# A new instruction order for a one-core attention, FFT and MLP kernel, with its last chunk finished in pieces

## The chip, the core and the metric

The kernel runs on one NeuronCore of a Trainium2 chip. The metric is the device time of one execution in microseconds (us). Engines: TensorE (PE in the profile; PEld is its weight loading), VectorE (DVE), ScalarE (ACT), GpSimd (POOL) and SyncE (SP), which here only issues transfers; "SPq" rows are SP issuing a DMA.

## The reference

Attention over 8 batches and 8 heads (576 positions, head size 64), then a mixing layer and an MLP on the result.

```python
scores = scale * np.matmul(q, k.transpose(0, 1, 3, 2))
mask_local = (rel >= 0) & (rel < 32)                       # heads 0 to 3
mask_strided = (rel >= 0) & (pos[None, :] % 32 == pos[:, None] % 32)   # heads 4 to 7
attn = softmax(np.where(mask, scores, -1e9)); attn_out = np.matmul(attn, v)
x = attn_out.transpose(0, 2, 1, 3).reshape(B, S, H * D)    # 8 x 576 x 512
u = x + np.real(np.fft.fft(np.fft.fft(x, axis=1), axis=2))
un = (u - mu) / np.sqrt(var + 1e-06)                       # over the last axis
return u + np.maximum(un @ w_ch1, 0.0) @ w_ch2             # 512 -> 2048 -> 512
```

## The kernel before, in words

**Attention.** The eight heads of a batch are four pairs; pairs 0 and 1 have the local mask, 2 and 3 the strided one. For each pair a load brings q and k (`qk5_0` is batch 5, pair 0) and the values; TensorE makes the scores (`s`, line 501 for a local pair, 54 small matmuls), DVE and ACT do the softmax, a DMA transpose on SP's queue turns the probabilities (`pT`, line 520, 18 blocks for a local pair), TensorE multiplies them with the values (`o`, lines 532 and 539), and the normalized result goes to `xd` in memory. When a batch's four pairs are there, `xa` loads a part of it back (line 998) and GpSimd gathers the rest by indirect DMAs (line 1002). Batch 0 works another way: its transposes are matmuls (line 754), and SP loads its inputs first of all (`q`, `mstr`, `mloc`, and the values `v` and `vlx`, `vsx`).

**Mixing.** Additions on DVE and GpSimd (`E`, `O`, `FD`, line 1010) and matmuls (`A`, `B`) make the FFTs. The result is normalized (`unp`) and turned by a DMA transpose (`uT`, line 1308).

**MLP.** The 4608 tokens are 18 chunks of 256, c0 to c17. A chunk has eight "ups": 24 matmuls of 128x256 into `ph` (line 1532), which ACT and GpSimd make into an fp16 high and low part. The "downs" (line 1658) are 96 matmuls of 128x512 into two accumulators, `acc`; DVE adds u to them (line 1666), and SP stores the rows (line 1675). The last four chunks make the downs from seven products instead of eight: 168 matmuls of 128x256 (line 1601) into `pa` and `pb`. There every up is followed by `hidden7`: relu on ACT (line 1564) into one of two `x` buffers, four 128x128 sums on DVE (line 1568, "hsum"), an fp16 copy on ACT (line 1575) and the rest of it on DVE (line 1578). `finish7` (lines 1608 to 1611) puts the seven products together: one ACT copy and eight DVE instructions, and then both stores.

**What sets the order.** Every engine carries out its instructions in the order in which they stand in the program, and a waiting instruction holds up all behind it. That order is laid out while the program is built, by a planner in the kernel (class `Order`). Steps are announced as `op(engine, duration, ...)`, with the buffers that they take (`get`) and give back (`put`), the events that they need, a bias and a slack. The planner takes the steps one after another by the time at which their engine could begin them and by their bias; steps with `alt` may go to DVE or GpSimd. SP has a model of its own: how long an issue takes of its queue, and when the transfer engines are free. The numbers that steer all this are the table `P`: biases by kind of step, slacks (`SLD2` is the slack ahead of `o`), `LX` and `LE` (what hsum and `E` on the second engine count extra), `ORD0` (batch 0's pairs in order), `vo` (which value loads of batch 0 stand behind which q load). Where the planner foresees idle TensorE while a PSUM tile for weight statistics is open, it puts in dummy matmuls (line 1381).

Of the kernel before, what the change touches and what calls it, by code (L numbers as in the profile page):

```python
# [11 lines left out]
F32 = mybir.dt.float32  # L12
# [3 lines left out]
AF = mybir.ActivationFunctionType  # L16
# [3 lines left out]
B, H, S, D = 8, 8, 576, 64  # L20

P = dict(
    WV0=0.228, ub=-187.36, SL2=0, SLD2=3.532, GL0=8, LAT=0.637, GL=9.0, t2=121.316, l0=-1127.679, a0=-807.088,
    sq0=-7.328, w00=-751.008, w01=-485.877, w02=-485.971, hold=398.589, c=-935.492, z=175.263, f0=-1280.172,
    w03=-170.758, s00=-640.699, s01=-730.715, s02=-653.813, s03=-436.694, w1=-58.299, s1=-408.163, p0=-1078.153,
    p1=-355.073, pn=-123.274, a1=-327.528, f1=-427.179, a2=80.128, f2=-74.138, an=258.341, fn=153.256, db=-50.784,
    up=323.728, dn=544.434, ev=154.438, WS=1.287, WV=0, WA=0.042, WG=21.908, WT=0, SL=0.222, SLD=0, np=3, AL=116.829,
    SG=57.917, Lcl=-4.074, Lfs=108.137, Lwl=68.096, Lul=-140.163, LO=-208.877, LE=-1.586, Lc2=108.104, LSD=-60.205,
    Lsub=100.369, Lsub0=83.995, Lrt=107.889, Lu=45.646, ORD0=(3, 1, 0, 2), vo=([], [2], [0, 1], [3]),
    S0=('qk', 'qk', 'kt', 'pt'),  # L30
    S1=('f6', 'f6', 'u', 'kt', 'u', 'f6', 'uT', 'u', 'u', 'uT', 'f6', 'f6', 'kt', 'f6', 'f6', 'qk'), HB=4, RB=1, X0=0,
    X1=0, X2=0, cs=187.891, T=-13.32, TQ=3, LT=71.249, LX=13.094, LH=-7.702, LF=27.454,
)
ORD0 = P["ORD0"]
FP32 = {(b, hp) for b in range(3) for hp in range(4)}
# [134 lines left out]
class Op:  # L170

    def __init__(self, engine, dur, get="", put="", need="", sets="", at=None, lat=None, n=1, slack=0.0, dma=0.0, note="", alt=None):
# [25 lines left out]
class Order:  # L200
# [38 lines left out]
    def run(self, until=None):  # L239
        while self.threads and until not in self.events:  # L240
# [44 lines left out]
                    self.cold = est + 3.6  # L285
                o.dur += min(o.dur, max(self.cold - est, 0.0) / 2)
            if o.engine == "S" and o.dur:
                self.free["S"] = est + 0.5 * o.n
                end = self.free["D"] = max(max(est + 1.3, self.free["D"]) + o.dur, est + 0.42 * o.n + 1.1)
            else:  # L290
                end = self.free[o.engine] = est + o.dur
                if o.engine in "VG" and pair(o):
                    h = self.held[o.engine]
                    h.append((est, end - 0.14))
                    del h[:-6]
                if o.dma:
                    end = self.free["D"] = max(est + 2.0, self.free["D"]) + o.dma
# [17 lines left out]
op = Op  # L315
# [3 lines left out]
def body(ctx: ExitStack, tc: tile.TileContext, a, out):  # L319
# [24 lines left out]
    def psbig(name):  # L344
        return big.tile([128, 1024], F32, tag="big", name=name)
# [77 lines left out]
    def att_pair(b, hp):  # L423
# [94 lines left out]
        yield op("S", 2.4 if local else 1.7, lat=2.4, get="pt", need="zv", put="qk" if local else "pbt", note=f"turn {nm}")  # L518
# [72 lines left out]
    def att_pair32(b, hp):  # L591
# [6 lines left out]
        end = yield op("S", 1.7, get="qk vsum" if hp == ORD0[0] else "qk", note=f"load {nm}")  # L598
# [665 lines left out]
    def norm(c, s, u, uT):  # L1264
# [42 lines left out]
        yield op("S", 0.9, put=ptag, sets=f"uT{nm}", note=f"uT {nm}")  # L1307
        nc.sync.dma_start_transpose(uT[:, :, 128 * s : 128 * s + 128], unp.rearrange("p x d -> p (x d)"))


# [150 lines left out]
    def xt(name):  # L1461
        return late_["p"].tile([128, 8, 128], F32, tag="x", name=name, bufs=2)
# [25 lines left out]
    class Chunk:  # L1488


        def __init__(self, c, keys):
            self.c, self.keys = c, keys
            self.h = {}
# [59 lines left out]
        def ups7(self):  # L1553
            c = self.c
            for fp in range(8):
                yield op("T", 2.61, get=("f6" if fp % 2 else "hq") + " ph", put="uT" if fp == 7 else "", sets=f"up{c}" if fp == 7 else "", at=0, note=f"up {c} {fp}", slack=SLD)
                spawn(self.hidden7(fp, self.up_products(fp)), bias=P["ev"])

        def hidden7(self, fp, ph):

            c = self.c
            yield op("A", 0.62, get="x", put="ph", note=f"relu {c} {fp}")
            X = xt(f"x{c}_{fp}")
            A.activation(X[:, 4:8].rearrange("p k t -> p (k t)"), ph, AF.Relu, scale=HS / 2)  # L1564
# [226 lines left out]
```

## Time and profile before

| | us |
|---|---|
| time, median of 3 runs (lowest, highest) | 958.61 (954.17, 961.56) |
| the profiled execution | 956.11 |
| its span | 954.3 |
| PE busy | 915.7 (96%) |
| DVE busy | 667.1 (70%) |
| ACT busy | 475.7 (50%) |
| POOL busy | 273.3 (29%) |

The span is what the trace covers; 1.8 us of the profiled execution lie outside it. TensorE is busy nearly throughout, so the table says little about what a changed order is worth: that stands in the places where TensorE waits, and in the stretches ahead of its first and behind its last product.

### The profile page before, as it was taken

How to read it: one execution, taken by the hardware profiler on the slowest of the kernel's cores; microseconds unless marked ns; L12 is line 12 of the kernel's file. 1: busy time of each engine (PE TensorE's matmuls, PEld its weight loads, DVE VectorE, ACT ScalarE, POOL GpSimd, SP SyncE). 2: the span in 40 equal slices, each digit the busy share in tenths (PEclk: the TensorE clock that was granted, in tenths of full speed). 3: DMA queues.
4: the chain of work that ended last, by engine and by line, in shares of the span. 5: the costliest groups of instructions: out<-in, count | busy, mean ns of one | idle time of the engine just before them, and what ended most of it. 6: DMA issues, size and time to landing. Idle time of an engine off the chain costs nothing.

```text
span 954.3 us, 24166 instructions
## 1 busy us (share of the span) xinstructions
PE 915.7 (96%) x10166; PEld 675.1 (71%) x10166; DVE 667.1 (70%) x1293; ACT 475.7 (50%) x883; POOL 273.3 (29%) x260
## 2 busy tenths in 40 slices
PE   7788999999999999999999999999999999999996
PEld 6666875757776667666766667666767767888885
DVE  4679877586875677569575687759665988657363
ACT  3468763446645546364744565455633454333331
POOL 0101242346422441346332551255224510000000
PEclk9999999999999999999999999999999999999998
DMA  9887562354325850564327451655142101101000
GB/s 284 294 325 268 175 169 81 87 152 123 112 47 124 176 129 29 123 166 95 97 48 164 104 165 21 168 133 138 31 93 78 34 12 40 23 23 45 2 23 23
DMA packets 131885, 105.50 MB, mean 111 GB/s; under 512 B 101089, under 2 KB 109697, under 8 KB 131777
## 3 DMA queue, kind: packets, MB, share of 16 engines
q1 hardware_dynamic: 129296, 95.84, 37.8%
q0 software_dynamic: 2480, 8.13, 3.1%
q8 instruction: 79, 1.29, 0.6%
q14 instruction: 30, 0.24, 0.1%
HBM read 65.23 MB, written 18.89 MB: 88 GB/s over the span
## 4 chain that ended last, share of the span: by engine, by line
PE 59%; DVE 4%; DMA 2%; issue 1%; ACT 1%; POOL 0%; DVEq 0%; ACTq 0%
PE acc L1658 19%; PE ph L1532 18%; PE ph L1549 9%; PE pa L1601 4%; PE pb L1601 3%; PE B L1118 1%; DMA pT<-qk 1%; PE A L1095 1%; PE s L501 1%; PE o L532 1%; DVE unp L1306 1%; PE o L539 1%; DVE tmp L1010 0%; PE A L1096 0%; DMA uT<-unp 0%
## 5 line engine op out<-in xcount | busy, mean ns | idle before, releaser
L1532 PE MATMUL ph<-uT,W 128*128 128x256 f16 x2688 | 308.7, 274 | 2.0 <-DMA uT<-unp 2.0
L1658 PE MATMUL acc<-W,h 128*128 128x512 f16 x1344 | 302.3, 379 | 3.2 <-DVE u L1666 3.2
L1532 PEld LDWEIGHTS <-W 128*128 128x128 f16 x2688 | 259.8, 98 | 40.7 <-DMA uT<-unp 2.1
L1637 POOL TENSOR_TENSOR h<-hf,h 128x512 f16<-128x512 f32 x112 | 142.9, 1276 | 331.0 <-ACT h L1635 247.4
L1658 PEld LDWEIGHTS <-h 128*128 128x128 f16 x1344 | 128.6, 98 | 147.8 <-issue 4.2
L1634 ACT ACTIVATE hf<-ph 128x512 f32<-128x512 f32 x112 | 66.4, 593 | 166.9 <-PE ph L1532 133.7
L1549 PE MATMUL ph<-uT,W 128*128 128x256 f16 x768 | 86.5, 273 | 0.0
L1549 PEld LDWEIGHTS <-W 128*128 128x128 f16 x768 | 75.1, 98 | 9.1
L1601 PEld LDWEIGHTS <-h 128*128 128x128 f16 x660 | 64.6, 98 | 8.8
L1275 POOL TENSOR_TENSOR rstd<-mv,negh 128x1 f32<-128x1 f32 x36 | 26.2, 730 | 149.2 <-DVE mv L1272 142.2
L1635 ACT ACTIVATE h<-ph 128x512 f16<-128x512 f32 x112 | 66.2, 591 | 0.3 <-DVE W L1349 0.3
L1568 DVE TENSOR_TENSOR x<-x 128x128 f32<-128x128 f32 x128 | 31.3, 287 | 34.0 <-ACT x L1564 32.9
L1306 DVE TENSOR_TENSOR unp<-un,unp 128x512 f16<-128x512 f32 x33 | 37.6, 1140 | 24.5 <-ACT unp L1303 24.5
L1578 DVE TENSOR_TENSOR h<-x,h 128x896 f16<-128x896 f32 x32 | 34.8, 1091 | 22.9 <-ACT h L1575 22.7
L1575 ACT CAST h<-x 128x896 f16<-128x896 f32 x32 | 30.0, 938 | 40.0 <-DVE x L1568 38.4
L1564 ACT ACTIVATE x<-ph 128x512 f32<-128x512 f32 x32 | 19.1, 597 | 49.8 <-PE ph L1549 47.1
L478 DVE SCALAR_TENSOR_TENSOR kt<-qk,sc,kt 128x576 f16<-128x576 f32 (+1 forms) x40 | 35.0, 915 | 9.3 <-ACT kt L463 9.3
L463 ACT ACTIVATE kt<-qk,sc 128x576 f16<-128x576 f32 (+1 forms) x40 | 29.3, 785 | 19.1 <-DVE sc L419 12.8
L1254 ACT ACTIVATE pq<-B,fcm 128x128 f32<-128x128 f32 (+7 forms) x105 | 27.2, 380 | 14.4 <-DVE rt L1244 9.5
L1303 ACT CAST unp<-un 128x512 f16<-128x512 f32 x33 | 20.4, 617 | 22.9 <-DVE un L1285 19.1
L1601 PE MATMUL pa<-T,h 128*128 128x256 f16 x192 | 31.4, 273 | 0.0
L1601 PE MATMUL pa<-W,h 128*128 128x256 f16 x184 | 30.5, 273 | 0.0
(298 smaller groups left out, 1352.6 us busy)
## 6 DMA issues: line engine op xcount, KB each, us to landing
qk<-in_qk SPq DMA_DIRECT2D x28, 592.0 KB
sa<-in_w SPq DMA_DIRECT2D x20, 512.0 KB
out<-u SPq DMA_DIRECT2D x32, 256.0 KB
W<-in_w SPq DMA_DIRECT2D x12, 512.0 KB
vn<-in_vl SPq DMA_DIRECT2D x10, 432.0 KB
xd<-xo SPq DMA_DIRECT2D x16, 256.0 KB
vn<-in_vs SPq DMA_DIRECT2D x10, 384.0 KB
xa<-xd SPq DMA_DIRECT2D x7, 512.0 KB
```

The costliest lines, as they stand in the source:

```text
L478: V.scalar_tensor_tensor(out=lo, in0=src, scalar=f, in1=hi, op0=ALU.mult, op1=ALU.subtract)
L1306: on(o).tensor_tensor(out=unp[:, 1], in0=un, in1=unp[:, 0], op=ALU.subtract)
L1532: T.matmul(ph[:, i, :], W1[:, 4 * (f0 // 512) + d, x, f0 % 512 : f0 % 512 + 128], self.uhl[y][:, d, :], start=(n == 0), stop=(n == 11))
L1549: T.matmul(ph[:, 256 * i : 256 * i + 256], W1[:, 4 * (f0 // 512) + d, x, f0 % 512 : f0 % 512 + 128], self.uhl[y][:, d, :], start=(n == 0), ...
L1568: on(o).tensor_tensor(out=X[:, k], in0=X[:, x], in1=X[:, y], op=f)
L1575: A.copy(h[:, 0], X[:, 0:7])
L1578: on(o).tensor_tensor(out=h[:, 1], in0=X[:, 0:7], in1=h[:, 0], op=ALU.subtract)
L1601: T.matmul(ps[:, 256 * q : 256 * q + 256], h[:, y, x], m(z), start=first and n == 0 and k == 6, stop=last and n == 2 and (k % 2 == 1 or k ...
L1634: A.activation(hf, ph, AF.Relu, scale=HS)
L1635: A.activation(hh, ph, AF.Relu, scale=HS)
L1637: G.tensor_tensor(out=hl, in0=hf, in1=hh, op=ALU.subtract)
L1658: T.matmul(self.acc[s], (hh, hl)[x][:, i, 128 * s : 128 * s + 128], W2[:, f, y, :], start=(f == 0 and n == 0), stop=(f == 15 and n == 2))
```

## The change

1. The planner's model of SP's queue: an op has a new argument `issue`, the time that it takes of the queue, 2.65 us for a local pair's transpose, 1.5 for a strided one's, 1.3 for `uT`, 2.2 for the two stores of a chunk; all others 0.55 us per DMA instead of 0.5. Some latencies are set too. No instruction comes from it directly.
2. A new table `P`. It changes the order on all engines. `SLD2` goes from 3.532 to 0. With `LX`, hsum moves from DVE to GpSimd in all 32 ups of the last four chunks (128 instructions); with `LE`, the five additions `E` of 128x1536 that GpSimd did go to DVE; with `X2`, batch 2's subtraction of the maximum is folded into its exponentials (40 small ACT instructions in place of a few on DVE). There are 254 dummy matmuls instead of 247; TensorE's other work is the same.
3. The last chunk: `downs_last` does its 168 products in another order, so that the sums that the output is made of come one after another, the last of them 24 matmuls. `finish_last` adds and stores them in pieces: rows 128 to 255 (256 KB), then the right half of rows 0 to 127 (128 KB), then their left half (128 KB).

```diff
 P = dict(
-    WV0=0.228, ub=-187.36, SL2=0, SLD2=3.532, GL0=8, LAT=0.637, ...
+    LTU=2.8, WV0=0.257, ub=-215.412, SL2=0.548, SLD2=0, GL0=8, LAT=0.637, ...
...
-    Lsub=100.369, Lsub0=83.995, Lrt=107.889, Lu=45.646, ORD0=(3, 1, 0, 2), vo=([], [2], [0, 1], [3]),
+    Lsub=85.755, Lsub0=62.935, Lrt=124.673, Lu=16.396, ORD0=(2, 0, 1, 3), vo=([], [], [], [0, 1, 2, 3]),
...
-    X1=0, X2=0, cs=187.891, T=-13.32, TQ=3, LT=71.249, LX=13.094, LH=-7.702, LF=27.454,
+    X1=0, X2=1, cs=216.454, T=-27.713, TQ=3, LT=102.806, LX=-45.064, LH=-18.9, LF=43.439,
...
+        self.issue = 0.55 * n if issue is None else issue
...
-                self.free["S"] = est + 0.5 * o.n
+                self.free["S"] = est + o.issue
...
-        yield op("S", 2.4 if local else 1.7, lat=2.4, get="pt", ..., note=f"turn {nm}")
+        yield op("S", 2.4 if local else 1.7, lat=2.4, issue=2.65 if local else 1.5, get="pt", ..., note=f"turn {nm}")
...
-            spawn(self.downs7() if self.seven else self.downs(), bias=P["dn"])
+            final = self.seven and c == len(chunks) - 1
+            spawn(self.downs_last() if final else self.downs7() if self.seven else self.downs(), bias=P["dn"])
...
+        def downs_last(self):
...
+            for i, (ks, fps) in enumerate((((0,), range(4)), ((1,), range(4)), ((2,), range(4)), ((3,), range(4)),
+                                           ((0, 1), range(4, 7)), ((2, 3), range(4, 7)), ((0, 1), (7,)), ((2, 3), (7,)),
+                                           ((4,), range(8)), ((5,), range(8)), ((6,), range(8)))):
...
+                for k in ks:
+                    products(k, fps)
+                if i == 6:
+                    spawn(self.finish_last(ps), bias=P["ev"])
+
+        def finish_last(self, ps):
...
+            yield op("V", 0.9, need=f"dc{c}", note=f"fin {c}")
+            stt(u1[:, hi], ps[4][:, lo], u1[:, hi])
+            stt(u0[:, hi], ps[4][:, lo], u0[:, hi])
+            yield op("S", 0.7, note=f"store {c}")
+            nc.sync.dma_start(rows(1, slice(0, 512)), u1)
+            yield op("V", 0.45, need=f"dd{c}", note=f"fin {c}")
+            stt(u0[:, hi], ps[5][:, lo], u0[:, hi])
+            yield op("S", 0.4, note=f"store {c}")
+            nc.sync.dma_start(rows(0, hi), u0[:, hi])
+            yield op("V", 0.45, need=f"de{c}", note=f"fin {c}")
+            stt(u0[:, lo], ps[6][:, lo], u0[:, lo])
+            yield op("S", 0.4, note=f"store {c}")
+            nc.sync.dma_start(rows(0, lo), u0[:, lo])
```

Three places of the order show what moves. The first is SP's queue at the start of the program, before:

```order
L697 DMA q_121<-in_qk 128x1184
L705 DMA mstr<-in_mstr 128x55
L708 DMA ident<-in_ident 128x128
L697 DMA q_123<-in_qk 128x1184
L701 DMA mloc<-in_mloc 128x480
L717 DMA vlx_84<-in_v 96x1170
L697 DMA q_125<-in_qk 128x1184
L717 DMA v_122<-in_v 128x780
L717 DMA v_124<-in_v 96x1170
L697 DMA q_126<-in_qk 128x1184
```

And now:

```order
L698 DMA q_121<-in_qk 128x1184
L706 DMA mstr<-in_mstr 128x55
L709 DMA ident<-in_ident 128x128
L698 DMA q_122<-in_qk 128x1184
L702 DMA mloc<-in_mloc 128x480
L698 DMA q_123<-in_qk 128x1184
L698 DMA q_125<-in_qk 128x1184
L714 DMA turns<-in_flip 128x129
L718 DMA vsx_85<-in_v 128x780
L718 DMA vlx_84<-in_v 96x1170
```

The fourth q load stood behind three value loads and now stands ahead of all of them; the two other value loads come behind these rows. The second place is SP's queue where batch 5's scores follow the end of batch 4 (`pT5_1` is the turned probabilities of batch 5, pair 1; `xa4` the reload of batch 4), before:

```order
L1675 DMA out_0<-u2_0_3789 128x512
L1675 DMA out_0<-u2_1_3894 128x512
L998 DMA xa4_6326<-xd4_109 128x2x512
L520 DMA_TRANSPOSE pT5_1_6504<-qk5_1_5993 128x18x128
L1308 DMA_TRANSPOSE uT8_6662<-unp8_0_6696 128x8x128
```

And now:

```order
L433 DMA qk5_1_6359<-in_qk 128x1184
L436 DMA vn5_1_6363<-in_vl 96x1152
L999 DMA xa4_6425<-xd4_109 128x2x512
L521 DMA_TRANSPOSE pT5_0_6495<-qk5_0_6086 128x18x128
L851 DMA xd5_110<-xo5_0_6665 128x4x128
```

In both a transpose stands right behind the reload; now it is pair 0's, and pair 1's loads stand ahead of the reload. On TensorE, `s5_1` and `o5_1` had 96 matmuls of the ups, 48 of the downs and another pair's scores between them; now there are 72 matmuls of the ups and 24 of the downs between `s5_0` and `o5_0`. The third place is the end of DVE's order, before:

```order
L1568 TENSOR_TENSOR x17_7_13824<-x17_7_13824 128x128 x4
L1578 TENSOR_TENSOR h17_7_13831<-x17_7_13824,h17_7_13831 128x896
L1610 SCALAR_TENSOR_TENSOR u7_0_11904<-pb17_13582,cout2_104,u7_0_11904 128x256
L1610 SCALAR_TENSOR_TENSOR u7_1_12019<-pb17_13582,cout2_104,u7_1_12019 128x256
L1611 TENSOR_TENSOR ev17_13897<-ev17_13897 128x256
L1611 TENSOR_TENSOR u7_0_11904<-u7_0_11904,ev17_13897 128x512
L1610 SCALAR_TENSOR_TENSOR ev17_13897<-pb17_13582,cout2_104,ev17_13897 128x256
L1611 TENSOR_TENSOR u7_0_11904<-u7_0_11904,ev17_13897 128x512
L1611 TENSOR_TENSOR u7_1_12019<-u7_1_12019,ev17_13897 128x512
L1611 TENSOR_TENSOR u7_1_12019<-u7_1_12019,ev17_13897 128x256
```

And now:

```order
L1580 TENSOR_TENSOR h17_7_13804<-x17_7_13773,h17_7_13804 128x896
L1623 TENSOR_TENSOR ev17_13867<-ev17_13867 128x256
L1623 TENSOR_TENSOR u7_0_12089<-u7_0_12089,ev17_13867 128x512
L1622 SCALAR_TENSOR_TENSOR ev17_13867<-pa17_13756,cout2_104,ev17_13867 128x256
L1622 SCALAR_TENSOR_TENSOR u7_1_12200<-pa17_13756,cout2_104,u7_1_12200 128x256
L1623 TENSOR_TENSOR u7_1_12200<-u7_1_12200,ev17_13867 128x512
L1622 SCALAR_TENSOR_TENSOR u7_1_12200<-pb17_13757,cout2_104,u7_1_12200 128x256
L1622 SCALAR_TENSOR_TENSOR u7_0_12089<-pb17_13757,cout2_104,u7_0_12089 128x256 x2
L1622 SCALAR_TENSOR_TENSOR u7_0_12089<-pc17_13758,cout2_104,u7_0_12089 128x256
```

All eight instructions of the finish came behind the chunk's last products; now only the last row does, which reads `pc`, the sum that comes last. The sums of line 1568 are gone from DVE.

## Rows read from the trace of the kernel before

**Rows 1.** Busy time by stretch: stretch, length, busy per engine (instructions), PE's granted clock, DMA share, GB/s.

```profile
0.00:130.00 130.00, 107.79 (x1509) 89.19 (x1510) 98.30 (x187) 79.37 (x128) 19.63 (x21) 0.97 0.80 261
130.00:946.00 816.00, 807.95 (x8659) 585.87 (x8657) 564.86 (x1100) 396.27 (x756) 253.72 (x239) 1.00 0.36 87
205.00:225.00 20.00, 17.68 (x173) 12.96 (x172) 16.37 (x28) 10.69 (x18) 11.01 (x11) 0.91 0.68 197
946.00:954.30 8.30, 0.00 (x0) 0.00 (x0) 3.90 (x8) 0.02 (x1) 0.00 (x0) 0.69 0.17 64
```

**Rows 2.** PE's waits: engine, line, for what; us in total, times, the longest.

```profile
PE acc L1658 <- DVE u L1666: 3.2, 4, 2.1
...
PE o L532 <- DMA pT<-qk: 2.4, 1, 2.4
PE ph L1532 <- DMA uT<-unp: 2.0, 1, 2.0
```

**Rows 3.** Timeline of the end: start, length, engine, line, instruction (idle before, releaser).

```profile
945.36 0.49 PE L1601 MATMUL pb<-W,h 128*128 128x256 f16 x3
945.89 0.88 DVE L1610 SCALAR_TENSOR_TENSOR u<-pb,cout,u 128x256 f32<-128x256 f32 x2 [4.90 <-PE pb L1601]
...
947.86 0.48 DVE L1610 SCALAR_TENSOR_TENSOR ev<-pb,cout,ev 128x256 f32<-128x256 f32 x1
948.26 1.74 DVE L1611 TENSOR_TENSOR u<-u,ev 128x512 f32<-128x512 f32 x3
948.97 1.39 SPq L1675 DMA_DIRECT2D out<-u  x2
```

**Rows 4.** Busy time by stretch, inside the last store's transfer.

```profile
951.00:951.50 0.50, 0.00 (x0) 0.00 (x0) 0.00 (x0) 0.00 (x0) 0.00 (x0) 0.50 1.00 389
```

**Rows 5.** Timeline of the start, on PE, DVE and SP.

```profile
18.05 0.91 PE L569 MATMUL s<-q 64*64 64x54 f32 x44 [1.34 <-DMA q<-in_qk]
...
27.72 0.96 DVE L855 TENSOR_TENSOR xo<-o,rs 128x768 f32<-128x768 f32 x1
...
34.30 1.28 SPq L898 DMA_DIRECT2D z<-xd  x3
```

**Rows 6.** Timeline of PE in batch 4, pair 1: from its scores to `o`.

```profile
313.51 0.83 PE L501 MATMUL s<-kt 64*64 64x96 f16 x54
314.27 5.41 PE L1532 MATMUL ph<-uT,W 128*128 128x256 f16 x48
...
319.55 5.34 PE L1658 MATMUL acc<-W,h 128*128 128x512 f16 x24
324.81 0.82 PE L501 MATMUL s<-kt 64*64 64x96 f16 x54
...
335.98 1.05 PE L532 MATMUL o<-vlx,pT 96*64 96x65 f16 x54 [2.40 <-DMA pT<-qk]
```

**Rows 7.** Timeline of SP's queue, and of PE at 211, around two transposes.

```profile
206.76 1.26 SPq L1308 DMA_TRANSPOSE uT<-unp  x1
...
211.08 3.23 PE L1532 MATMUL ph<-uT,W 128*128 128x256 f16 x18 [1.98 <-DMA uT<-unp]
...
318.13 0.39 SPq L998 DMA_DIRECT2D xa<-xd  x1
...
322.05 5.25 SPq L520 DMA_TRANSPOSE pT<-qk  x1
```

**Rows 8.** The page's costliest groups: line, engine, instruction, count, busy us, mean ns, idle before.

```profile
L1568 DVE TENSOR_TENSOR x<-x 128x128 f32<-128x128 f32 x128 | 31.3, 287 | 34.0 <-ACT x L1564 32.9
...
L1578 DVE TENSOR_TENSOR h<-x,h 128x896 f16<-128x896 f32 x32 | 34.8, 1091 | 22.9 <-ACT h L1575 22.7
L1575 ACT CAST h<-x 128x896 f16<-128x896 f32 x32 | 30.0, 938 | 40.0 <-DVE x L1568 38.4
L1564 ACT ACTIVATE x<-ph 128x512 f32<-128x512 f32 x32 | 19.1, 597 | 49.8 <-PE ph L1549 47.1
```

**Rows 9.** GpSimd's instructions of line 1010: count, shortest/median/longest ns, first and last start, form.

```profile
L1010 POOL TENSOR_TENSOR E<-FD x14: 721/800/1838, 166.2 to 744.9; 128x257 f32<-128x257 f32 x14
...
L1010 POOL TENSOR_TENSOR E<-xa,xb x5: 3424/3428/4255, 144.0 to 643.4; 128x1536 f32<-128x1536 f32 x5
```

More of the change, by code (lines that the diff above doesn't have):

```diff
@@ L170, with __init__ @@
 class Op:
-    def __init__(self, engine, dur, get="", put="", need="", sets="", at=None, lat=None, n=1, slack=0.0, dma=0.0, note="", alt=None):
+    def __init__(self, engine, dur, get="", put="", need="", sets="", at=None, lat=None, n=1, slack=0.0, dma=0.0, note="", alt=None, issue=None):
+        self.issue = 0.55 * n if issue is None else issue
         self.alt = {engine: (dur, 0.0), **{e: d if isinstance(d, tuple) else (d, AL) for e, d in alt.items()}} if alt else None
@@ L517, in att_pair @@
         V.scalar_tensor_tensor(out=lo, in0=sm, scalar=PSC, in1=hi, op0=ALU.mult, op1=ALU.subtract)
-        yield op("S", 2.4 if local else 1.7, lat=2.4, get="pt", need="zv", put="qk" if local else "pbt", note=f"turn {nm}")
+        yield op("S", 2.4 if local else 1.7, lat=2.4, issue=2.65 if local else 1.5, get="pt", need="zv", put="qk" if local else "pbt", note=f"turn {nm}")
         pt = apool.tile([128, 2 * NQB, 128], F16, tag="pt", name=f"pT{nm}", bufs=1)[:, 0 : 2 * NQB if local else 2 * NG2]
@@ L597, in att_pair32 @@
         vt = (vlf if local else vsf)[0]
-        end = yield op("S", 1.7, get="qk vsum" if hp == ORD0[0] else "qk", note=f"load {nm}")
+        end = yield op("S", 1.7, lat=2.4, get="qk vsum" if hp == ORD0[0] else "qk", note=f"load {nm}")
         qk = apool.tile([128, S + KP], F32, tag="qk", name=f"qk{nm}", bufs=2)
@@ L1224, in placed @@
         else:
-            yield op("S", 0.4, n=4, get="ux" if b % 2 == 0 else "", put="f6 f6", sets=f"u{b}b0 u{b}b1" + (f" ux{b // 2}" if b % 2 else ""), note=f"ux {b}")
+            yield op("S", 0.4, n=4, issue=2.4, get="ux" if b % 2 == 0 else "", put="f6 f6", sets=f"u{b}b0 u{b}b1" + (f" ux{b // 2}" if b % 2 else ""), note=f"ux {b}")
             nc.sync.dma_start(us[b, "b", 0][0:1], dst[0][32:33])
@@ L1306, in norm @@
         on(o).tensor_tensor(out=unp[:, 1], in0=un, in1=unp[:, 0], op=ALU.subtract)
-        yield op("S", 0.9, put=ptag, sets=f"uT{nm}", note=f"uT {nm}")
+        yield op("S", 0.9, lat=P["LTU"], issue=1.3, put=ptag, sets=f"uT{nm}", note=f"uT {nm}")
         nc.sync.dma_start_transpose(uT[:, :, 128 * s : 128 * s + 128], unp.rearrange("p x d -> p (x d)"))
@@ L1555, in ups7 @@
             for fp in range(8):
-                yield op("T", 2.61, get=("f6" if fp % 2 else "hq") + " ph", put="uT" if fp == 7 else "", sets=f"up{c}" if fp == 7 else "", at=0, note=f"up {c} {fp}", slack=SLD)
+                yield op("T", 2.61, get=("f6" if self.in_f6(fp) else "hq") + " ph", put="uT" if fp == 7 else "", sets=f"up{c}" if fp == 7 else "", at=0, note=f"up {c} {fp}", slack=SLD)
                 spawn(self.hidden7(fp, self.up_products(fp)), bias=P["ev"])
@@ L1578, in hidden7, with in_f6, products @@
             on(o).tensor_tensor(out=h[:, 1], in0=X[:, 0:7], in1=h[:, 0], op=ALU.subtract)
+        def in_f6(self, fp):
+            return fp < 6 if self.c == len(chunks) - 1 else fp % 2 == 1
+        def downs_last(self):
+            c = self.c
+            side = lambda k, half: lambda fp, y: W2[:, 2 * fp + k, y, 256 * half : 256 * half + 256]
+            tt = lambda k: lambda fp, y: TT[fp][:, y, k]
+            start = {0: W2[:, 1:17:15, 0, 0:256], 2: TT[0][:, 0, 2:5:2]}
+            parts = (6, side(1, 0)), (1, tt(1)), (2, tt(2)), (5, tt(3)), (0, tt(0)), (3, side(0, 1)), (4, side(0, 0))
+            ps = {}
+            def products(k, fps):
+                x, m = parts[k]
+                for fp in fps:
+                    h = self.h[fp]
+                    for n, (y, z) in enumerate(W3):
+                        if fp == 0 and n == 0 and k in start:
+                            T.matmul(ps[k].rearrange("p (a t) -> p a t", a=2), h[:, y, x], start[k], start=True, stop=False)
+                        else:
+                            o = ps[k // 2 * 2][:, 256 * (k % 2) : 256 * (k % 2) + 256] if k < 4 else ps[k][:, 0:256]
+                            T.matmul(o, h[:, y, x], m(fp, z), start=k >= 4 and fp == 0 and n == 0, stop=fp == 7 and n == 2 and (k % 2 == 1 or k >= 4))
+            for i, (ks, fps) in enumerate((((0,), range(4)), ((1,), range(4)), ((2,), range(4)), ((3,), range(4)),
+                                           ((0, 1), range(4, 7)), ((2, 3), range(4, 7)), ((0, 1), (7,)), ((2, 3), (7,)),
+                                           ((4,), range(8)), ((5,), range(8)), ((6,), range(8)))):
+                need = " ".join(f"h{c}_{fp}" for fp in fps) + f" t2_{max(fps)} t2_z" + (f" down{c - 1}" if i == 0 else "")
+                yield op("T", 0.33 * len(ks) * len(fps), get="big big acc" if i == 0 else "", need=need, sets=f"d{'xxxxxxabcde'[i]}{c}", at=0, note=f"down {c} {i}", slack=0.3)
+                if i == 0:
+                    pa, pb = psbig(f"pa{c}"), psbig(f"pb{c}")
+                    ps.update({0: pa[:, 0:512], 2: pa[:, 512:1024], 4: pb[:, 0:512], 5: pb[:, 512:1024], 6: pacc.tile([128, 512], F32, tag="acc0", name=f"pc{c}")})
+                for k in ks:
+                    products(k, fps)
+                if i == 6:
+                    spawn(self.finish_last(ps), bias=P["ev"])
@@ new lines, in finish_last @@
+        def finish_last(self, ps):
+            c = self.c
+            u0, u1 = self.u[0], self.u[1]
+            lo, hi = slice(0, 256), slice(256, 512)
+            stt = lambda out, q, x: V.scalar_tensor_tensor(out=out, in0=q, scalar=cout2, in1=x, op0=ALU.mult, op1=ALU.add)
+            add = lambda out, x, y: V.tensor_tensor(out=out, in0=x, in1=y, op=ALU.add)
+            rows = lambda s, cols: out[256 * c + 128 * s : 256 * c + 128 * s + 128, cols]
+            yield op("A", 0.65, get="x", note=f"ev {c}")
+            ev = xt(f"ev{c}").rearrange("p (k a) t -> p k (a t)", k=4)
+            A.activation(ev[:, 0:2], ps[0].rearrange("p (k t) -> p k t", k=2), AF.Copy, scale=cout2)
+            yield op("V", 1.1, note=f"fin {c}")
+            add(ev[:, 1], ev[:, 1], ev[:, 0])
+            u0k = u0.rearrange("p (k t) -> p k t", k=2)
+            add(u0k, u0k, ev[:, 0:2])
+            yield op("V", 1.6, need=f"db{c}", note=f"fin {c}")
+            stt(ev[:, 1], ps[2][:, lo], ev[:, 1])
+            stt(u1[:, lo], ps[2][:, hi], u1[:, lo])
+            u1k = u1.rearrange("p (k t) -> p k t", k=2)
+            add(u1k, u1k, ev[:, 1:2].to_broadcast([128, 2, 256]))
+            yield op("V", 0.9, need=f"dc{c}", note=f"fin {c}")
[11 more added lines that the diff above has]
+            nc.sync.dma_start(rows(0, lo), u0[:, lo])
@@ L1672, in store @@
             put = "ux ux" if kinds[0] else ("u u" if self.keys[0][1] == "b" else "")
-            yield op("S", 1.4, n=2, put=put, note=f"store {self.c}")
+            yield op("S", 1.4, n=2, issue=2.2, put=put, note=f"store {self.c}")
             for s in range(2):
```

20 lines of the change are left out of this document (10 added, 10 removed).

## The prediction

> **What bounds the kernel now.** I read the busy time by stretch first, because a new order can win only where TensorE waits. TensorE is busy for 915.7 of 954.3 us; of the 38.6 us that are left, 22.2 lie in the first 130 us, 8.1 in the 816 us that follow, and 8.3 behind the last product [rows 1]. A fourth place is not idle time: from 205 to 225 us the granted clock averages 0.91, so the records there lie partly at 1.2 instead of 2.4 GHz; 0.09 of 20 us makes 1.8 us. It falls around the wait for a turned `uT` [rows 1, 2]. So the change can win about 40 us if all of it went, and no more, because TensorE's products are the same. Then I read the list of waits: the middle's 8.1 us are a few single waits, 3.2 for DVE to free the accumulators, 2.4 for one probability transpose, 2.0 for one `uT` [rows 2]. Then the timelines of the end, the start and the two transposes.
>
> **The end.** The last product ends at 945.36 + 0.49 = 945.85. DVE then works from 945.89 to 950.00, eight instructions in one chain, and the span ends 4.3 us later, with the second of two stores [rows 3]. After the change one instruction of 128x256 stands behind the last product, of the form that took 0.48 us [rows 3], and one store. DVE thus ends 0.04 + 0.48 = 0.5 us after the last product instead of 4.15: -3.6. Of the 4.3 us behind it a part is the two stores' issues, 1.39 for both, and the transfer, which moves at 389 GB/s [rows 3, 4]: 256 KB in 0.67 us, 128 KB in 0.34. I take -0.3 for the smaller transfer and nothing for the issue, since the second issue alone stands on the path in both cases. Together **-3.9 us** (-3.4 to -4.4). What must cover it: the last hidden part must be ready before its products come. Between the last up and the first products that need it stand 48 + 36 = 84 products, by 5.28 us for 48 [rows 6] 9.2 us. The chain beside it is relu 0.60, hsum, copy 0.94 and rest 1.09 [rows 8]. With hsum at 1.8 us (below) that is 4.4; because three ups come in a row and there are only two `x` buffers, some 2 us of queueing come on top. About 3 us are left.
>
> **hsum on GpSimd.** No row shows these instructions there. From below: `E` of 128x257 took 721 ns at its shortest, 128x1536 took 3428 [rows 9]; the line through both gives 2.12 ns an element and 0.45 us for 128 elements. From above: the 257 form took 1838 ns at its longest. Four in a row make 1.8 us, or at most 7.4; I take 1.8, because the slope is that of the same operation and type and only single ones of the 14 are long. The DVE form takes 4 x 0.287 = 1.15 us [rows 8]. The `x` buffer is then held for 4.4 instead of 3.8 us. Two ups and the 42 products between them take (48 + 42) x 0.110 = 9.9 us, and each `x` serves one up of two: free. The Trainium skill (SBUF — State Buffer, "Who interferes with whom") says that a DVE instruction with two inputs in SBUF and a GpSimd instruction that reads SBUF block each other for a whole instruction, which speaks against this move, because line 1578 on DVE is such a one; the 1838 beside 721 ns of the same form agrees. By that rule one hsum in each up would lose up to 1.09 us, a hold of 5.5 us. That leaves the sum as it is and takes 1 of the 3 us of cover at the end. The five `E` on DVE lie among work that TensorE does not wait for: nothing.
>
> **The start.** The fourth pair's scores wait 1.34 us for their q, until 18.05 [rows 5]. By the sizes in the order 4.05 MB of loads stood up to its end, now 2.75; at 261 GB/s, the mean until 130 us [rows 1], it comes 5 us earlier. But the values come later by as much, all loads together are the same, and the last `o` needs values and q. Then the last `xo` ends at 28.68, the reload `z` is issued at 34.30, and until then SP stores in its own order [rows 5]; by hand I get `z` at 32.6, -1.7. From there to 130 us the transfers run at 0.80 of their engines and DVE is busy 98.3 of 130 us [rows 1], so a part of that is given back. And the plan itself holds seven more dummy matmuls, which says that it foresees as much idle time as before. I take **-1 us** (-4 to +3).
>
> **The middle.** The slack ahead of `o` in the plan falls from 3.53 us to zero. Batch 4's stalled pair shows the chain: scores at 313.51, transpose issued at 322.05, `o` at 335.98 [rows 6, 7]: 8.5 us, then 13.9 us to landing. This transpose stands behind an `xa` issued 3.9 us earlier, and its issue alone took 5.25 us [rows 7]. From below, `uT` landed 211.08 - 206.76 = 4.3 us after its issue, with 8 blocks instead of 18 [rows 7]; an undisturbed one of 18 I put at 6. In the new order the shortest distances between scores and `o` are: batch 5 pair 0, one set of scores 0.76, 72 ups' and 24 downs' products, 0.76 + 72 x 0.110 + 24 x 0.219 = 13.9 us [rows 6]; batch 4 pair 0 14.7; batches 3 and 6 pair 0 16.6. Before, all but one of the pairs from batch 3 on had over 20. With a landing after L us the waits are L - 5.4, L - 6.2 and twice L - 8.1: at L = 6 together 0.6, at L = 13.9 together 27.8. All four transposes stand right behind or near an `xa`, as the stalled one did; but the reload may be long over when the transpose is issued. I take L of 8 for batch 5 (2.6) and 7 to 8 for the others, **+4** in sum. Against that the 2.4 us of batch 4's old pair go, I take half of the waits for accumulators and `uT` as gone (where the longest of these waits was, 2.6 us of products stood between a chunk's last accumulation and the next one's first; the new order has 2.7 at the least), -2.6, and half of the lost clock, -0.9. The middle is **-2 us** (-9 to +25).
>
> **Sum.** -3.9 - 1 - 2 = -6.9: 956.1 becomes 949.2. The profiled execution lies 2.5 us below the median of 958.6, so against the median it is 951.7. I predict 951. One per cent is 9.6 us: about what a measurement here can tell from no change.
>
> **Rivals.**
> (a) The order takes out nearly all waits: the end -3.9, the start -4, the middle with its clock -8: -15.9, 940 to 943 us. For it: each single wait has a place and the queue's times are now those of the trace. Against it: distances became shorter, not longer. Chance 0.20.
> (b) Only the end counts, the middle trades one wait for another: -3.9, 952 to 955 us. It lies in the forecast's own range. The forecast and this together 0.62.
> (c) Slower: `o` waits for transposes behind `xa`. If those of batches 4, 5 and 6 land as batch 4's did, 13.9 us after issue, they wait 7.7 + 8.5 + 5.8 = 22.0; less the 2.4 removed +19.6, with end and start +14.7: 971 to 973 us. If it is batches 5 and 6 alone, 963 to 966. The point from which it decides: landings of more than 9 us in three of them eat up what the end gives. For it: one row that shows it, and no slack any more. Against it: an `xa` that was issued earlier. Chance 0.12, of which two thirds are slower by over 1%.
> (d) GpSimd's sums are as long as `E`'s longest forms: hsum of 4 to 7 us holds `x`, TensorE waits in the last four chunks by 1 to 4 us each time that three or four ups stand in a row, and the cover at the end is gone. Then the end's gain is lost: 955 to 962 us. Chance 0.06.
>
> **Numbers.** Of the forecast's and (b)'s 0.62, which spread over 946 to 957 us, a fifth falls below 949.0; with most of (a) that is 0.31 for faster by over 1%. Slower by over 1%, above 968.2, is (c)'s larger form with a little for mishaps at the start: 0.10. Within 1%: 0.59. The range goes from 942, which takes in part of (a), to 961, which takes in (d) and leaves out most of (c).
>
> **What would show it.** The end: last product to the end of the span at 4.3 to 4.9 us instead of 8.5, with one DVE instruction between, and no wait of TensorE in the last 168 products. hsum on GpSimd: about 0.45 us each; 0.7 and more speaks for (d). The start: first fold product before 39 us and the fourth pair's scores near 14. The middle: waits of `o` for `pT` in batches 3 to 6, each with its transpose near an `xa`; their sum under 5 us for the forecast, near zero for (a), over 14 for (c). The forecast is wrong if idle time between 130 and 940 us leaves 3 to 14 us, or if TensorE's products in the first 130 us end more than 4 us off.

## The result and the profile after

The changed kernel takes 950.05 us (median of 11 runs, 947.72 to 951.49), against 958.61 us (954.17 to 964.47, 11 runs): ratio 0.990, 95% interval 0.9879 to 0.9921. The prediction was 951 us. The profiled execution took 948.91 us with a span of 947.0, 7.3 us less than before's 954.3. The median fell by 8.6, and the runs lie closer together: 3.8 us from the lowest to the highest, before 10.3.

The busy time by stretch, to be laid beside [rows 1] (stretch, length, PE, PEld, DVE, ACT and POOL busy, PE's granted clock, DMA share, GB/s):

```profile
0.00:130.00 130.00, 107.37 (x1412) 89.64 (x1416) 92.95 (x174) 77.08 (x125) 22.35 (x21) 0.95 0.75 250
205.00:225.00 20.00, 20.00 (x234) 14.72 (x231) 9.32 (x26) 9.46 (x19) 7.42 (x13) 1.00 0.84 215
130.00:938.00 808.00, 805.01 (x8717) 584.36 (x8715) 534.77 (x991) 403.15 (x795) 305.59 (x362) 1.00 0.35 90
938.00:947.00 9.00, 5.01 (x46) 4.25 (x44) 2.57 (x6) 0.00 (x0) 0.00 (x0) 0.90 0.16 59
```

Three places changed, and one of them the wrong way. **The middle:** TensorE's idle time between 130 us and its last product went from 7.9 to 3.0 us, and the clock of 0.91 between 205 and 225 us is back at 1.00, which made 1.8 us: -6.7. **The end:** the timeline of the last 10 us (start, length, engine, line, instruction, idle before and releaser):

```profile
940.23 2.78 PE L1603 MATMUL pc<-W,h 128*128 128x256 f16 x24
940.43 1.40 DVE L1622 SCALAR_TENSOR_TENSOR u<-pb,cout,u 128x256 f32<-128x256 f32 x3 [1.67 <-PE pb L1603]
940.94 0.33 SPq L1641 DMA_DIRECT2D out<-u  x1
941.85 0.33 SPq L1645 DMA_DIRECT2D out<-u  x1
943.05 0.48 DVE L1622 SCALAR_TENSOR_TENSOR u<-pc,cout,u 128x256 f32<-128x256 f32 x1 [1.23 <-PE pc L1603]
943.56 0.33 SPq L1649 DMA_DIRECT2D out<-u  x1
```

The last product ends at 943.01, one DVE instruction at 943.53, and the span at 947.0: 3.99 us behind the last product where [rows 3] show 8.45: -4.5. **The start** lost what remains: the spans differ by 7.3, so by these two profiles the start is about 3.9 us longer. Its rows, on SP's queue and TensorE:

```profile
26.20 1.06 SPq L1330 DMA_DIRECT2D W<-in_w  x2
...
29.06 5.49 SPq L865 DMA_DIRECT2D xd<-xo  x6
...
35.92 1.52 SPq L899 DMA_DIRECT2D z<-xd  x3
```

```profile
41.42 0.70 PE L912 MATMUL fold0a<-z,turns 128*128 128x257 f32 x2 [2.67 <-DMA z<-xd]
```

The last `o` of batch 0 ends at 24.5 us, 2.7 us earlier than before, and the last `xo` at 26.2 instead of 28.7. But the six last stores now take 5.49 us to issue instead of 2.54, and `z` goes out at 35.92 instead of 34.30 [rows 5]. On TensorE the loss shows as 0.4 us more idle time in the first 130 us, 20.8 instead of 18.3 us of dummy matmuls, and a granted clock of 0.95 instead of 0.97.

What TensorE waited for (us, times, longest), beside [rows 2]: the `uT` wait is gone, and one `pT` wait of 0.8 us is left.

```profile
PE fold0a L912 <- DMA z<-xd: 2.7, 1, 2.7
...
PE acc L1729 <- DVE u L1737: 1.4, 1, 1.4
...
PE o L533 <- DMA pT<-qk: 0.8, 1, 0.8
```

### The profile page after: what moved, and what is told of

It is laid out like the page before. It is cut to its first block, busy times and chain, and to the rows that moved or that the text cites. A ratio compares the mean times of both kernels' runs of the same rounds, so it can differ in the third digit from the quotient of the medians.

```text
span 947.0 us, 24248 instructions
## 1 busy us (share of the span) xinstructions
PE 917.4 (97%) x10170; PEld 678.2 (72%) x10173; DVE 630.3 (67%) x1169; ACT 480.2 (51%) x919; POOL 327.9 (35%) x383
## 4 chain that ended last, share of the span: by engine, by line
PE 90%; DMA 4%; DVE 3%; ACT 1%; issue 1%; SPq 0%; ACTq 0%; DVEq 0%
PE ph L1534 31%; PE acc L1729 30%; PE ph L1551 9%; PE pa L1672 3%; PE pb L1672 2%; PE B L1119 2%; PE s L502 2%; DMA W<-in_w 2%; PE A L1096 2%; PE pa L1603 1%; PE o L533 1%; DMA turns<-in_flip 1%; PE o L540 1%; DMA xd<-xo 1%; PE t L639 1%; DMA sa<-in_w 1%
## 5 line engine op out<-in xcount | busy, mean ns | idle before, releaser
L1708 POOL TENSOR_TENSOR h<-hf,h 128x512 f16<-128x512 f32 x112 | 146.4, 1307 | 335.7 <-ACT h L1706 258.7
L1729 PEld LDWEIGHTS <-h 128*128 128x128 f16 x1344 | 128.9, 98 | 143.5 <-issue 1.7
L1570 POOL TENSOR_TENSOR x<-x 128x128 f32<-128x128 f32 x128 | 67.9, 552 | 85.9 <-ACT x L1566 83.4
L1672 PEld LDWEIGHTS <-h 128*128 128x128 f16 x495 | 48.4, 98 | 6.6
L1307 DVE TENSOR_TENSOR unp<-un,unp 128x512 f16<-128x512 f32 x33 | 30.6, 926 | 31.7 <-ACT unp L1304 31.7
L479 DVE SCALAR_TENSOR_TENSOR kt<-qk,sc,kt 128x576 f16<-128x576 f32 (+1 forms) x40 | 32.4, 850 | 5.4 <-ACT kt L464 4.9
L1245 DVE TENSOR_TENSOR rt<-pq 128x257 f32<-128x257 f32 (+1 forms) x42 | 17.8, 464 | 18.3 <-ACT pq L1255 18.1
L1286 DVE TENSOR_SCALAR un<-u,mv,rstd 128x512 f32<-128x512 f32 x30 | 17.2, 574 | 13.5 <-POOL rstd L1276 13.1
```

The lines of the kernel that those rows point to most:

```text
L479: V.scalar_tensor_tensor(out=lo, in0=src, scalar=f, in1=hi, op0=ALU.mult, op1=ALU.subtract)
L1672: T.matmul(ps[:, 256 * q : 256 * q + 256], h[:, y, x], m(z), start=first and n == 0 and k == 6, stop=last and n == 2 and (k % 2 == 1 or k ...
L1708: G.tensor_tensor(out=hl, in0=hf, in1=hh, op=ALU.subtract)
L1729: T.matmul(self.acc[s], (hh, hl)[x][:, i, 128 * s : 128 * s + 128], W2[:, f, y, :], start=(f == 0 and n == 0), stop=(f == 15 and n == 2))
```

## The experiments

Two kernels leave the planner as it is and swap the last chunk alone. Two more (`new_order_again`, `new_order_third`) are the changed kernel itself, run again. In all others the planner's own sequence of steps was written out as a list (`SEQ`, one entry per step, with its engine: T, V, A, G, S for TensorE, DVE, ACT, GpSimd, SP) and the program carried out from it, so that everything but the named entries keeps its place; each diff is one of that list, with other entries left out. All ratios are to the kernel before, run beside them.

**The two halves of the change.** `old_order_new_tail` is the kernel before with `downs_last` and `finish_last`; `new_order_old_tail` the changed kernel with:

```diff
-            final = self.seven and c == len(chunks) - 1
+            final = False
...
-            return fp < 6 if self.c == len(chunks) - 1 else fp % 2 == 1
+            return fp % 2 == 1
```

> The old order with the new last chunk alone. Theory (the end is worth about 4.4 us by itself, as the changed kernel's trace shows 3.99 us from the last product to the end of the span against 8.45): a span some 4.4 us shorter, ratio 0.995 to 0.996, and no wait of TensorE within the last chunk's products. Rival (the end's gain depends on hsum being on GpSimd, because with hsum on DVE the last hidden part comes late): TensorE waits 1 us or more before the last chunk's products and the ratio is 0.997 or more.

> The new order with the old last chunk: what the order alone brings. Theory (start loses about 3 us, the middle wins about 6): 2 to 4 us faster than before, ratio 0.996 to 0.998, with about 8.4 us behind the last product. Rival (the order alone brings nothing and the end brings all): ratio 1.000.

Measured: the tail alone 0.9966 (0.9945 to 0.9987), the order alone 0.9947 (0.9927 to 0.9966). Their product is 0.9913, the whole change 0.990, so the halves add up within the noise. The tail alone gave a little less than expected, though its interval covers the expected 0.995 to 0.996; its span ends 4.5 us behind the last product. The profile of the order alone still has the old end, here DVE's last instructions and the stores:

```profile
942.61 0.88 DVE L1681 SCALAR_TENSOR_TENSOR u<-pb,cout,u 128x256 f32<-128x256 f32 x2 [3.44 <-PE pb L1672]
...
944.99 1.74 DVE L1682 TENSOR_TENSOR u<-u,ev 128x512 f32<-128x512 f32 x3
945.70 1.39 SPq L1746 DMA_DIRECT2D out<-u  x2
```

With a span of 950.6 that is 8 us behind the last product. The rival that the end needs hsum on GpSimd falls: in the old order, with hsum on DVE, TensorE did not wait within the last products. The order alone won 5.1 us in the ratio (3.3 to 7.0), more than the 2 to 4 us expected.

**hsum on DVE again.**

```diff
-G|hsum 14 0
+V|hsum 14 0
...
```

(the same for all 32). 

> The new order, step by step the same, with the 32 hsum steps on DVE instead of GpSimd. Theory (hsum is off the path on either engine): the same time as the changed kernel within 1 us, 4 x 0.29 us for one hsum, no wait of TensorE after 800 us. Rival (the move to GpSimd is what keeps the new end free of waits): TensorE waits in the last four chunks, 2 us or more slower than the changed kernel.

Measured 948.38 us, 0.9889 (0.985 to 0.9927); the changed kernel beside it 948.25 us, 0.9881 (0.9846 to 0.9916) (`new_order_again`). 

> The changed kernel once more, beside the next two, which are compared with it: 0.990 of before (0.988 to 0.992), about 1.5 to 3 us above the early weight load's time.

No difference. In the changed kernel hsum reads so (shortest/median/longest ns, from when to when), and with hsum on either engine TensorE is busy for all of the 140 us from 800 to 940 (the changed kernel's row by stretch):

```profile
L1570 POOL TENSOR_TENSOR x<-x x128: 444/455/1301, 784.6 to 928.8; 128x128 f32<-128x128 f32 x128
```

```profile
800.00:940.00 140.00, 140.00 (x1277) 124.72 (x1275) 59.56 (x87) 48.28 (x65) 62.17 (x117) 1.00 0.10 23
```

**Why the start lost.** In the changed kernel the load of weight pieces 4 and 5 stands between the stores of batch 0's pairs; before, it stood ahead of three of them (SP's entries alone; `ld 0 4` is the load, `xd0 2` the stores of pair 2).

```diff
 S|xd0 2
+S|ld 0 4
 S|xd0 0
-S|ld 0 4
 S|xd0 1
 S|xd0 3
```

> The new order, step by step the same, with the weight load of pieces 4 and 5 (512 KB) moved ahead of the stores of batch 0's pair 0 on SP's queue, the place that it had before. Theory (this load, between the stores, holds the last stores up and so the reload z): z is issued at 33 to 34 instead of 35.9 us, the first fold product starts at 39 to 39.8 instead of 41.4, and 1.5 to 3 us of it reach the end: 0.988 to 0.989 of before. Rival (the weights set the start, z is not what is waited for): z early, but the end the same as the changed kernel's, 0.990 to 0.992.

Its timeline, on SP and TensorE:

```profile
22.47 1.60 SPq L1476 DMA_DIRECT2D W<-in_w  x2
...
28.51 3.04 SPq L1011 DMA_DIRECT2D xd<-xo  x6
...
32.97 1.51 SPq L1045 DMA_DIRECT2D z<-xd  x3
```

```profile
38.33 0.70 PE L1058 MATMUL fold0a<-z,turns 128*128 128x257 f32 x2 [1.83 <-DMA z<-xd]
```

The six stores issue in 3.04 instead of 5.49 us, `z` goes out 2.95 us earlier, and the span is 943.7, 3.3 us shorter. The stores' issue separates the kernels in every profile kept: 2.5 to 2.7 us in the five of the old order, 4.1 to 5.8 in the five of the new order with the load in its new place, 3.0 to 3.3 in the four with the early load. So where the load stands is the cause of the slow issue. `z` itself scatters more: the same changed kernel, run twice more, issued it at 34.31 and 35.87, and on the mean of those profiles it is 35.4 with the load in its new place and 33.9 with the early load, so about 1.5 of the 2.95 us are the load's. The time was 947.65 us, 0.9892 (0.9868 to 0.9916). To compare it directly both were run once more on one chip:

> The changed kernel again, as the measure for the two below on one chip: 0.988 to 0.991 of before.

> The early weight load again, beside the changed kernel. Theory (the reload z comes 3 us earlier and it all reaches the end): its median 1.5 to 3.5 us below the changed kernel's of this call. Rival (the three us in the profile were luck): within 1 us of it.

The changed kernel 948.99 us, 0.9886 (0.9865 to 0.9907); the early load 947.12 us, 0.9872 (0.985 to 0.9894), with spans of 948.5 and 945.9. The medians say 1.9 us, within the expected 1.5 to 3.5, but the intervals overlap: the mechanism is shown, its worth in the median lies between nothing and some 3 us. Its ratio is the lowest of all versions that were run.

**Two attempts to go on.** Behind `z`, TensorE waits for mixing steps on DVE that stand behind the weights' low parts (`wlo`), and the clock falls (with the early load: a wait of 1.66 us up to 60.2 us, a granted clock of 0.52 from 60 to 65 us). `gram` is TensorE's part of the weight statistics, `SD257` and `A3` are mixing steps. `new_order_start2` has the early load and:

```diff
 V|SD0 0
-V|wlo 0 2
-V|wlo 0 3
 ...
 V|SD257 0
+V|wlo 0 2
+V|wlo 0 3
 ...
-T|gram 0 8
 ...
 T|A3 0
+T|gram 0 8
```

> The new order with the early weight load, and two more steps moved in the first 70 us: DVE's low parts of weight pieces 2 and 3 (2.48 us) go behind the mixing's second set of additions, and TensorE's statistics of piece 8 go behind the mixing's third matmul step. Theory (TensorE waits there for DVE, and the clock falls to 1.2 GHz behind the wait): the waits of 1.9 and 1.7 us before those steps go, the granted clock stays at 2.4 GHz between 57 and 66 us, and 2 to 5 us more than by the early load alone reach the end: 0.984 to 0.987 of before. Rival (from there to 130 us DVE and the weights' preparation set the pace): the waits come back later in the first 130 us, and the time is that of the early load, 0.987 to 0.990.

It won nothing: 950.89 us, 0.9906 (0.9872 to 0.994), at the median 2.6 us above the changed kernel beside it (948.25) and above what either theory or rival gave; against the early load, which ran on another chip, the intervals overlap. Its profile is of its slowest execution (954.18 us). The wait of 1.9 us only shrank to 1.51, and the time moved into the next step that needs DVE (TensorE's timeline):

```profile
57.84 0.73 PE L1287 MATMUL A<-f32c,FD 128*128 128x290 f32 x2 [1.51 <-DVE FD L1134]
...
63.33 0.63 PE L1520 MATMUL gram<-W 128*128 128x128 bf16 x8 [2.30 <-DVE W L1496]
65.72 1.03 PE L1520 MATMUL gram<-W 128*128 128x128 bf16 x8 [1.76 <-DVE W L1496]
...
75.66 2.01 PE L1327 MATMUL B<-f32b,AT 127*128 127x254 f32 x4
```

The last row took 1.08 us in the changed kernel: behind the two waits the granted clock is at 1.2 GHz (0.50 from 65 to 75 us) until 77 us. `new_order_start3` left TensorE's order alone and spread the two low parts:

```diff
-V|wlo 0 2
-V|wlo 0 3
 ...
 V|c3 0 10
+V|wlo 0 2
 ...
 V|ulo 0_1
+V|wlo 0 3
```

> The early weight load, and on DVE the low parts of weight pieces 2 and 3 moved one each to two later places, behind the statistics' input of pieces 8 to 11 and behind the first chunk's low part, so that nothing that TensorE waits for stands behind them; TensorE's order is left alone. Theory (in the run that failed, DVE's 2.48 us only moved from one waiting product to the next): both waits near 57 and 60 us shrink by about 2 us, the low clock behind them stays away, 2 to 4 us less than the early load. Rival (weights and DVE's sum of work set the pace until 90 us): the first ups start no earlier than with the early load, the same time within 1 us.

It took 948.9 us, 0.9892 (0.9872 to 0.9912), no better than the changed kernel beside it (948.99). DVE, now free, waits for ACT, and ACT prepares weights too (DVE's and ACT's timelines):

```profile
57.66 0.42 DVE L1131 TENSOR_TENSOR FD<-fold0a,E 128x254 f32<-128x254 f32 x1 [1.85 <-ACT FD L1124]
```

```profile
55.03 1.12 ACT L1487 ACTIVATE W<-W 128x1024 f32<-128x1024 f32 x1
56.06 1.11 ACT L1489 ACTIVATE W<-W 128x1024 int32<-128x1024 uint32 x1
57.07 0.34 ACT L1121 COPY E<-fold0a 128x254 f32<-128x254 f32 x1
...
57.52 0.17 ACT L1124 COPY FD<-fold0b 128x1 f32<-128x1 f32 x1
```

So neither move won time, and in both a wait for DVE came back. That between 50 and 90 us the weights' preparation on DVE and ACT sets the pace, as the rivals say, fits this, but only these waits show it: no run took work off the two engines.

**What the middle won.** The old order, with the two waits of [rows 2] for transposes taken away:

```diff
-S|ux 1
 ...
 S|uT 2_1
+S|ux 1
 ...
-S|xa 3
-G|xb 3
 ...
 S|turn 4_1
+S|xa 3
+G|xb 3
```

> The old order, step by step the same, with two transfers let past others on SP's queue: the second uT of chunk 2 goes ahead of four stores of batch 1, and batch 4's pT goes ahead of the xa reload and its gathers. Theory (what the middle wins is these two waits and the clock that falls after the first): the uT wait goes from 2.0 to about 0.4 us, the pT wait from 2.4 to 0, the clock from 205 to 225 us stays near 1.00 instead of 0.91, together 5 to 6 us, ratio 0.994 to 0.995. Rival 1 (the clock falls for another reason): 3.5 to 4 us, clock still 0.91. Rival 2 (the transposes are late whatever stands ahead of them): both waits stay, ratio 1.000.

(`ux` are stores, `xa` and `xb` a reload and its gathers, `turn` is a probability transpose.) Both waits went, and in this profile the clock stayed at 1.00 from 205 to 225 us, and yet there was no gain: 959.77 us, 1.0012 (0.9993 to 1.0031). TensorE's waits and its timeline tell why:

```profile
PE acc L1804 <- DVE u L1812: 4.2, 4, 2.0
...
PE s L647 <- issue: 2.1, 5, 0.5
```

```profile
208.59 0.67 PE L647 MATMUL s<-kt 64*64 64x96 f16 x45 [0.33 <-DVE kt L624]
209.62 0.29 PE L647 MATMUL s<-kt 64*64 64x96 f16 x4 [0.36 <-issue]
210.39 0.21 PE L647 MATMUL s<-kt 64*64 64x96 f16 x1 [0.48 <-issue]
```

At the place of the `uT` wait there are now stalls within the scores for which the trace shows no releaser; the same stalls, at 207 to 210 and 415 to 416 us, are in the profile of `old_order_new_tail`, where nothing was done in this stretch and neither the `uT` nor the `pT` wait occurs. The stretch from 205 to 225 us is no better for it (this run, then `old_order_new_tail`):

```profile
205.00:225.00 20.00, 18.08 (x179) 12.70 (x177) 15.98 (x27) 10.20 (x17) 11.99 (x12) 1.00 0.85 209
```

```profile
205.00:225.00 20.00, 18.22 (x171) 12.99 (x170) 15.76 (x22) 11.23 (x19) 11.82 (x11) 0.91 0.71 205
```

Nor does the clock follow the `uT` wait: it is 0.91 here in three profiles without that wait, that of `old_order_three` below, with the same two turns, among them. So the waits that I had read in one execution of the kernel before are not those of every execution. What both later profiles of the old order share is a wait near 560 us, where DVE frees the accumulators late. It was 0.18 and 2.06 us in before's profile and is 1.75 and 2.17 in that of `old_order_new_tail`, 2.02 and 1.23 in this one. So that place was tried, alone and with the two turns:

```diff
+V|fin 8
+V|fin 8
 V|O 5
 ...
-V|fin 8
 ...
-V|fin 8
```

> The old order with the two turns let past as in the run before, and chunk 8's two finish steps on DVE moved ahead of three of batch 5's mixing additions. Theory (what the two turns won was given back near 560 us, where DVE frees the accumulators late): the waits of 2.0 and 1.2 us there and the low clock behind them go, the span is 951 to 954 instead of 957.8 us, ratio 0.993 to 0.997. Rival (the time comes back once more at another place, because many places have little slack): another wait of TensorE of 2 us or more further on, ratio 0.998 to 1.002.

> The old order with chunk 8's finish moved ahead of the mixing's additions alone, without the two turns let past. Theory (this is the one place of the three that is waited for in most executions): 0.995 to 0.998, as with all three. Rival (it takes all three together): 0.999 to 1.001.

All three: 956.74 us, 0.9971 (0.995 to 0.9993). The finish alone: 956.17 us, 0.9958 (0.9943 to 0.9973). Its profile is of its slowest execution (959.11 us), whose `z` went out only at 37.25; in its timeline the accumulation follows the ups at once:

```profile
556.81 5.40 PE L1678 MATMUL ph<-uT,W 128*128 128x256 f16 x48
562.05 2.75 PE L1804 MATMUL acc<-W,h 128*128 128x512 f16 x12
```

This one place is worth some 3 to 4 us in the old order, and the two turns nothing. In the new order its counterpart is not there: of its waits for accumulators one is left, 1.4 us, the same in all nine profiles of that order.

All profiles kept show the middle together. From 130 us to the last product TensorE was idle for 7.9 to 8.6 us in the three of the old order whose finish of chunk 8 was not moved (6.1 and 6.5 where it was), and the low clock cost 1.7 to 3.5 us more in each of the five; in the nine of the new order it was idle for 2.9 to 4.2 us, and the clock stayed at 1.00. From 205 to 225 us it was busy for 17.7 to 18.2 us in each profile of the old order, by the one wait or by the stalls, and for all 20 us in each of the new. So against the first three the middle wins 5 to 9 us whichever executions are compared, although the single waits change.

## Why the prediction was right

The sum was right (949.2 forecast for the profiled execution, 948.91 measured), but two of its three terms were not: the start was mis-signed and the middle too small, and the two errors, +4.9 and -4.7 us, cancel. That they cancel is luck. Two of the forecast's own signs say so: the first fold product came at 41.42 instead of before 39 us, and the idle time between 130 and 940 us, 2.99 us, lies on the edge of the 3 to 14 beyond which it called itself wrong.

- **The end**, -3.9 forecast, -4.5 measured. DVE's part came as worked out (0.52 us behind the last product). Mis-sized was the last store: from DVE's end to the end of the span 3.5 instead of 4.3 us, where I had taken 0.3 off.
- **hsum**, 0.45 us each from the line through two other forms, measured 0.455 at the median (0.53 on the mean, 67.9 us for 128, the longest 1.30). That it costs nothing is shown by putting it back.
- **The start**, -1 forecast, +3.9 measured. The fourth pair's scores came 4.9 us earlier (13.12 instead of 18.05), as worked out. The step that failed is "by hand I get `z` at 32.6": the sum has no term for the six stores, which took 5.49 instead of 2.54 us to issue. Moving one load gave 32.97, in the repeat 34.16. The +3.9 is a reading of two executions, and before's had the quickest start of its order: by what TensorE still had to do at 130 us (the last product's end less 130, less the idle time and what the low clock cost), four profiles of the old order have 806.2 to 807.7 us left and the fifth 811.1, the five of the new order without the early load 808.9 to 810.9, so that the start loses 2 to 3 us on the mean.
- **The middle**, -2 forecast, -6.7 measured. The term that failed is the landing of the transposes, L of 7 to 8, which made +4. The shortest distance, batch 5 pair 0, did cause a wait, of 0.82 us (SP's queue, then TensorE's scores and `o`):

```profile
422.32 0.39 SPq L999 DMA_DIRECT2D xa<-xd  x1
433.83 2.69 SPq L521 DMA_TRANSPOSE pT<-qk  x1
```

```profile
423.57 0.88 PE L502 MATMUL s<-kt 64*64 64x96 f16 x54
...
438.42 1.05 PE L533 MATMUL o<-vlx,pT 96*64 96x65 f16 x54 [0.82 <-DMA pT<-qk]
```

  Landing took 438.42 - 433.83 = 4.6 us. By that alone no wait was due; it came because the way from the scores to the issue took 433.83 - 423.57 = 10.3 us, where I had taken 8.5 from batch 4. "Right behind `xa`" in the order was 11.5 us behind it in time. That was the argument against rival (c), and it holds: I had read nearness from the order, which has no times. In the nine profiles of the new order this wait is 0.5 to 2.0 us, and it is the only one for a `pT`. The waits for accumulators and `uT` fell from 5.2 to 1.4 us and the lost clock to nothing, where I had taken half of each.
- **Rivals.** (a) had the end and most of the middle right (-3.9 and -8, measured -4.5 and -6.7) and fails by the start alone; (b) and (c) fall with the middle; (d) falls with hsum.

What the middle won is shown by its size in all profiles, its cause only in part: 3 to 4 us lie at one place near 560 us, as an edit in the old order shows, and some 2 us with the lost clock lie between 205 and 225 us, where no edit was found that wins them. Why the runs of the new order scatter less stays open.

## What to carry to other kernels

A list of waits from one execution is a sample: a wait of 2 us that one profile shows may be missing in the next, so before one is removed it should be looked up in a second profile; the same holds for a sum of terms read from two profiles, as the start shows. When a step is moved past a load on a transfer queue, count how long the stores behind it take to issue, not only when their data is ready. And where two engines prepare something in the same stretch, moving one engine's share away from the waiting product may only bring the wait to the next, as it did in both tries here.

## What was not expected of the hardware

**Which engine starts first decides who waits.** Near 556 us DVE does two additions `FD` of 128x192, each with two inputs, and GpSimd an instruction `h`. In the kernel before, DVE's pair was over 0.21 us before GpSimd began (DVE's, GpSimd's and TensorE's rows):

```profile
556.02 0.61 DVE L1010 TENSOR_TENSOR FD<-tmp 128x192 f32<-128x192 f32 x2
556.56 1.05 DVE L517 SCALAR_TENSOR_TENSOR qk<-sm,qk 128x864 f16<-128x864 f32 x1
```

```profile
556.84 1.79 POOL L1637 TENSOR_TENSOR h<-hf,h 128x512 f16<-128x512 f32 x1 [2.35 <-DVE FD L1010]
```

```profile
558.32 1.46 PE L1658 MATMUL acc<-W,h 128*128 128x512 f16 x6 [0.18 <-DVE u L1666]
```

In `old_order_new_tail`, with the same order up to there, DVE came 0.34 us later and GpSimd 0.25 earlier, so that GpSimd's began while DVE's pair ran:

```profile
556.36 1.59 DVE L1010 TENSOR_TENSOR FD<-tmp 128x192 f32<-128x192 f32 x2
```

```profile
556.59 1.15 POOL L1707 TENSOR_TENSOR h<-hf,h 128x512 f16<-128x512 f32 x1 [1.76 <-issue]
```

```profile
559.64 1.46 PE L1728 MATMUL acc<-W,h 128*128 128x512 f16 x6 [1.75 <-DVE u L1736]
```

DVE's pair takes 1.59 instead of 0.61 us; GpSimd's takes 1.15 instead of 1.79, which it took beside DVE's next instruction, of line 517. TensorE waits 1.75 instead of 0.18 us: 0.98 of the difference is the longer pair, the rest the earlier shift of 0.59. In the three other profiles of the old order the pair took 1.58 us as well. This is what the Trainium skill (SBUF — State Buffer, "Who interferes with whom") says: a DVE instruction with two inputs in SBUF and a GpSimd one that reads SBUF exclude each other for a whole instruction, and the order of issue decides. The trace agrees; it also shows how a shift of half a microsecond between two engines becomes a longer wait of TensorE in one execution than in another.

**Stalls within the scores.** In the four later profiles of the old order, TensorE stops five or six times by 0.25 to 0.5 us, 2.1 to 2.6 us in all, mostly behind the 43rd to 53rd of the 54 score matmuls of a pair, with no releaser in the trace; in that of the kernel before the scores at 417 us run through. In the nine profiles of the new order there are two such stops of the 64x96 scores at most. What causes it stays open.
